# One up-weight load moved behind a token transpose, and eight matmul groups reordered to match, in a SwiGLU feed-forward kernel

## The chip, the core and the metric

The kernel runs on one core of a Trainium2 chip. The metric is device time in microseconds (us) of one execution; before the change it is 115.72 us, the median of 3 runs (115.47 to 116.23). Times inside the kernel are read from one profiled execution; "at 10.5" means 10.5 us after the start of its span.

## What is computed

```python
x: (1, 2048, 512)   w_gate, w_up: (512, 1376)   w_down: (1376, 512)   all bf16
def reference(x, w_gate, w_up, w_down):
    g = jax.nn.silu(x @ w_gate)
    u = x @ w_up
    return (g * u) @ w_down
```

## The kernel before

**Tiles.** The 2048 tokens are cut into 4 chunks of 512 (chunk 0 is tokens 0-511, chunk 1 is 512-1023). The 1376 hidden columns are 10 F tiles of 128 (F tile 0 to 9) and a rest of 96. A *group* is one PSUM bank: one F tile of one chunk, gate or up. In a *classic* pair (`classic`, L469) the gate group and the up group of an F tile are computed directly: ScalarE (ACT) takes silu of the gate bank into `sg_sb`, VectorE (DVE) multiplies it with the up bank into `h_sb`. In the first part such a group is 8 matmuls (L424), two 64-column halves for each of four 128-row slices of D, run as pairs side by side.

**Strassen part.** Most of the remaining work is done in units (`Unit`) of two F tiles by two chunks with seven products instead of eight (Winograd's form of Strassen's method). For these, sums and differences of weight blocks (`ss_sb`, `w_sums`, L545, on GpSimd, called POOL) and of token blocks (`tt_sb`, `x_sums`, L575, four sums T1 to T4) are needed. `tt0` is for chunks 0 and 1 and is made on DVE, in four instructions of about 1.2 us, each behind the one before. `ss_sb` sums of F tile pairs 2, 4 and 3 are made on POOL, each pair behind the last, and the first behind T4. A cast of one block (A22, and B22 of the tokens) runs on ACT (L541). Of the third pair, the cast on ACT waits for the last weight sum of that pair on POOL.

**Loads.** All loads are issued by SyncE (SP) in the order of the `load` calls: `load_w` (L267) brings a slab of two F tiles of gate or up weights, 256 KB; `load_x` (L279) is a DMA that transposes tokens into `xT_sb`, here 256 tokens, 256 KB at a time. The first loads are: x of tokens 0-255 (untransposed), gate slab 0-1 (`wg0`), x of 256-511 (`x0b`), up slab 0-1 (`wu0`), gate slab 2-3 (`wg2`), up slab 2-3 (`wu2`), then x of 512-767 (`x1a`) and 768-1023 (`x1b`). Each load has a semaphore of its own; those that matter here are dma21 (`wu0`), dma29 (`wg2`), dma20 (`wu2`), dma0 and dma1 (`x1a`, `x1b`), dma12 and dma28 (gate and up slab 4-5).

**What sets the order.** The program is written as a list of operations with reads and writes; `Plan.schedule` gives each operation to an engine. PE's and SP's operations keep the order in which they are written. Those of ACT, DVE and POOL are taken by a simulated list schedule, earliest possible start first, so their order depends on the estimated landing time of each load (`.land` in `load`) and on estimated costs. The result is a fixed order on each engine; at run time an engine waits at the head of its own queue.

**Around the change.** After the gates and ups of F tiles 0 and 1 of chunk 0, PE runs `classic(0, [2, 3])` (gate 2, gate 3, up 2, up 3 of chunk 0), then `classic(1, [ft])` for F tiles 0, 1 and 2 of chunk 1, then the rests of 96 columns (`plan_x` L488, `plan_y` L514), one more classic pair (L435), and the units (L616 and L628). The first group that reads chunk 1 is also the first that needs `x1a` and `x1b`; T1 on DVE needs them as well.

Of the kernel before, what the change touches and what calls it, by code (L numbers as in the profile page):

```python
# [168 lines left out]
def bass_standalone__swiglu_ffn__prompt_kernel(nc, x, w_gate, w_up, w_down, out):  # L169
    _, S, D = x.shape  # L170
    F = w_gate.shape[1]
    P = 128
# [26 lines left out]
    with ExitStack() as es:  # L199
# [40 lines left out]
        def take(i):  # L240
            rest.remove(i)
            return i
# [7 lines left out]
        plan = Plan()  # L250
        engines = {"P": nc.tensor, "S": nc.sync, "A": nc.scalar, "D": nc.vector, "G": nc.gpsimd}

        landed = 2700

        def load(name, emit, writes, busy, lag):
            nonlocal landed
            landed += lag
            i = take(homes[name] if name in homes else rest[0])
            plan.add("S", emit, writes=writes, busy=busy, lag=1800, dma=(i, 16)).land = landed + (300 if landed < 10500 else 1600)

        slabs = [(0, 2), (2, 4), (4, 6), (6, 8), (8, NFF + 1)]
        slab_of = {ft: a for a, b in slabs for ft in range(a, b)}

        def load_w(name, src, m, c0, f0, f1):
            load(
                name,
                lambda e: e.dma_start(  # L267
                    w_sb[:, :, m, c0:c0 + f1 - f0], src[:, f0:f1].rearrange("(k p) f -> p k f", p=P)
                ),
                [name], 600, 3.7 * (f1 - f0),  # L270
            )

        def load_slab(a, b):
            load_w(f"wg{a}", w_gate, 0, a * P, a * P, min(b * P, F))
            load_w(f"wu{a}", w_up, 1, a * P, a * P, min(b * P, F - 32))

        def load_x(name, t0, t1):
            load(
                name, lambda e: e.dma_start_transpose(xT_sb[:, :, t0:t1], xf[t0:t1, :]), [name], 1500, 4 * (t1 - t0)  # L279
            )  # L280

        load(
            "xn",
            lambda e: e.dma_start(
# [4 lines left out]
        load_w("wg0", w_gate, 0, 0, 0, slabs[0][1] * P)  # L289
        load_x("x0b", HT, SC)  # L290
        load_w("wu0", w_up, 1, 0, 0, slabs[0][1] * P)
        load_slab(*slabs[1])
        for i in range(2):
            load_x(f"x1{'ab'[i]}", SC + i * HT, SC + (i + 1) * HT)
        load_slab(*slabs[2])
        load_slab(*slabs[4])
        load_w("wut", w_up, 0, F, F - 32, F)
# [16 lines left out]
        for i in range(2):  # L314
            load(
                f"wdy{i}",
                lambda e, i=i: e.dma_start(wdt_sb[2 * R * i:2 * R * (i + 1), 0, :], w_down[NFF * P:F - R, :]),
# [12 lines left out]
        def silu_op(out, src, reads, writes, prio=5, busy=A_BUSY):  # L330
            return plan.add(
                "A", lambda e: e.activation(out, src, ACT.Silu), reads, writes, busy, A_LAG, prio  # L332
            )

        def tt_op(engs, out, a, b, alu, reads, writes, prio, busy, after=()):
            return plan.add(
                engs, lambda e: e.tensor_tensor(out, a, b, alu), reads, writes, busy,  # L337
                G_LAG if engs == "G" else D_LAG, prio, after=after,
            )
# [5 lines left out]
        def pe(emit, reads, writes, n, step=PE_STEP, after=()):  # L345
            return plan.add("P", emit, reads, writes, int(n * step), PE_LAG, dma=None, after=after)
# [60 lines left out]
        def next_bank():  # L407
            nonlocal n_group
            b = turn[n_group % NB]
            n_group += 1  # L410
            return b

        def x_keys(c):
            if c == 1:
                return ["x1a", "x1b"]
            if c:
                return [f"x{c}"]
            return [("x0a", dk) for dk in range(KD)] + ["x0b"]

        def gu_emit(m, ft, c, b, dks, n0, n1):  # L420
            def emit(e):
                for dk in dks:
                    for h in (0, HC):
                        ins = e.matmul(  # L424
                            psum[h:h + HC, b, n0:n1], lhsT=w_sb[:, dk, m, ft * P + h:ft * P + h + HC],
                            rhs=xT_sb[:, dk, c * SC + n0:c * SC + n1], start=(dk == 0), stop=(dk == KD - 1),
                            tile_position=(0, h),
                        )
                return ins
            return emit  # L430

        def gu_whole(m, ft, c, b):
            def emit(e):
                for dk in range(KD):
                    ins = e.matmul(  # L435
                        bank(b), lhsT=w_sb[:, dk, m, ft * P:(ft + 1) * P], rhs=xT_sb[:, dk, c * SC:(c + 1) * SC],
                        start=(dk == 0), stop=(dk == KD - 1),
                    )
                return ins
            return emit  # L440

        def gu_group(m, ft, c, b, whole=False):
            emit = gu_whole(m, ft, c, b) if whole else gu_emit(m, ft, c, b, range(KD), 0, SC)
            pe(emit, x_keys(c) + [f"w{'gu'[m]}{slab_of[ft]}"], [("b", b)], KD)
# [3 lines left out]
        def ring(name, tiles):  # L448
            n = rings.get(name, 0)
            rings[name] = n + 1  # L450
            i = n % len(tiles)
            return tiles[i][:, :], (name, i)

        def hview(ft, c):
            return (h0_sb, h1_sb)[c // 2][:, ft, c % 2 * SC:(c % 2 + 1) * SC]
# [8 lines left out]
        def classic_out(ft, c, bg, bu):  # L464
            sg, ksg = ring("sg", sg_sb)
            silu_op(sg, bank(bg), [("b", bg)], [ksg])
            tt_op("D", hview(ft, c), sg, bank(bu), ALU.mult, [ksg, ("b", bu)], [("h", ft, c)], 5, D_BUSY)

        def classic(c, fts, own=None):  # L469
            gates = [next_bank() for ft in fts] if own is None else own[:1]  # L470
            ups = [next_bank() for ft in fts] if own is None else own[1:]
            for ft, b in zip(fts, gates):
                gu_group(0, ft, c, b, own is not None)
            for ft, b in zip(fts, ups):
                gu_group(1, ft, c, b, own is not None)
            for ft, bg, bu in zip(fts, gates, ups):
                classic_out(ft, c, bg, bu)
# [61 lines left out]
        def cast_op(eng, out, src, reads, writes, prio, busy, after):  # L539
            plan.add(  # L540
                eng, lambda e: e.activation(out, src, ACT.Copy) if eng == "A" else e.tensor_copy(out, src),  # L541
                reads, writes, busy, A_LAG if eng == "A" else G_LAG, prio, after=after,
            )
# [31 lines left out]
        def x_sums(pi, eng, prio, after):  # L575

            c0, c1 = 2 * pi, 2 * pi + 1
            xk = x_keys(c0) + x_keys(c1)
            key = lambda n, k: ("tt", pi, X_SUM[n], k)
            last, first = after, None  # L580
            for n in ("T1", "T2", "T3", "T4"):
                behind = last
                last = []
                for k0, k1 in [(0, KH)] if pi == 0 else [(k, k + 1) for k in range(KH)]:
                    block = lambda k, c: xT_sb[:, k * KH + k0:k * KH + k1, c * SC:(c + 1) * SC]
                    at = lambda n: tt_sb[pi][:, X_SUM[n], k0:k1, :]
                    rd = lambda n: at(n).bitcast(FP32)
                    B11, B12, B21, B22 = (block(k, c) for k in range(2) for c in (c0, c1))
                    a, b, of_ = {
                        "T1": (B12, B11, ()), "T2": (B22, rd("T1"), ["T1"]),  # L590
                        "T3": (B22, B12, ()), "T4": (B21, rd("T2"), ["T2"]),
                    }[n]
                    last.append(tt_op(
                        eng, at(n), a, b, ALU.subtract, xk + [key(o, k) for o in of_ for k in range(k0, k1)],
                        [key(n, k) for k in range(k0, k1)], prio, 1160 if eng == "D" else 1250, behind,
                    ))
                first = first or last
            for k in range(KH):
                cast_op("A", tt_sb[pi][:, X_SUM["B22"], k, :], xT_sb[:, KH + k, c1 * SC:(c1 + 1) * SC], xk, [key("B22", k)], 8, A_BUSY, first if pi else ())
            return last  # L600
# [414 lines left out]
        units = [(pi, u) for pi in range(2) for u in U_ORDER[pi]]  # L1015
        early = [2 * u + i for u in range(NFF // 2) if u not in U_ORDER[0] for i in range(2)]
        sums = w_sums(0, 8, (), "A", True)
        classic(0, [2, 3])
        for ft in early[:3]:
            classic(1, [ft])  # L1020
        sums = x_sums(0, "D", 4, sums)
        for u in U_ORDER[0]:
            sums = w_sums(u, 2, sums, "A")
# [69 lines left out]
```

## Time and profile before

| quantity | value |
|---|---|
| median of the runs | 115.72 us |
| the profiled execution | 115.52 us |
| its span, first to last instruction | 114.2 us |
| outside the span | 1.3 us |
| PE busy | 110.7 us |
| DVE busy | 76.5 us |
| ACT busy | 64.0 us |
| POOL busy | 62.2 us |
| granted TensorE clock | 1.000 |

An engine's busy time is a sum over stages. The profile's chain of waits follows, from the last instruction backwards, what released each step; the waits list tells who stood idle for whom. In a row of the timeline stand start, busy time, engine, line, operation, tiles and count, and in brackets the idle time ahead of it with what ended it. A busy PE in this trace may still be a waiting one: a matmul whose operand is late shows as a longer piece, since its neighbours' modelled ends cover the gap.

### The profile page before, as it was taken

The page shows a single profiled execution, that of the slowest core. Times are in us where ns is not written, and L with a number is a line of the kernel's source. Part 1 is how long each engine was busy: PE and PEld are TensorE (multiplying, and loading weights), DVE is VectorE, ACT ScalarE, POOL GpSimd, SP SyncE. Part 2 cuts the span into 40 slices and gives each one's busy share as a digit, 9 for nine tenths or more (in the row PEclk, how much of TensorE's full clock was granted, in tenths as well). Part 3 has the DMA queues.
Part 4 walks back from the last instruction along what each step waited for, and adds up shares of the span by engine and source line. Part 5 has one row for each costly group of instructions (what it writes and reads, how often), then busy time and mean ns, then how long its engine had stood idle before and what let it go on. Part 6 is the DMA issues. An engine that isn't in the chain of part 4 may idle for free.

```text
span 114.2 us, 1765 instructions
## 1 busy us (share of the span) xinstructions
PE 110.7 (97%) x646; PEld 68.0 (60%) x654; DVE 76.5 (67%) x113; ACT 64.0 (56%) x123; POOL 62.2 (54%) x61
## 2 busy tenths in 40 slices
PE   7999999999999999999999999999999999999993
PEld 2665555456674858576776858653344557866452
DVE  0113799883956858493948668499999957486423
ACT  5344765866679895867678786740567960000000
POOL 1493004999999999999998999845000000000000
PEclk9999999999999999999999999999999999999999
DMA  3999999994000000000000000000031002227976
GB/s 101 235 276 237 321 190 225 271 361 101 0 0 0 3 0 3 0 0 6 0 3 0 0 0 0 0 0 0 17 127 46 0 0 46 46 52 183 201 200 197
DMA packets 22808, 9.84 MB, mean 86 GB/s; under 512 B 12848, under 2 KB 22672, under 8 KB 22800
## 3 DMA queue, kind: packets, MB, share of 16 engines
q1 hardware_dynamic: 20656, 8.69, 31.5%
q10 hardware_dynamic: 2144, 1.05, 3.2%
q8 instruction: 5, 0.08, 0.3%
q14 instruction: 3, 0.02, 0.1%
HBM read 4.75 MB, written 2.10 MB: 60 GB/s over the span
## 4 chain that ended last, share of the span: by engine, by line
PE 96%; DVE 1%; issue 1%
PE psum L616 32%; PE psum L726 15%; PE psum L628 12%; PE psum L424 11%; PE psum L864 10%; PE psum L876 4%; PE psum L488 3%; PE psum L754 3%; PE psum L350 2%; PE psum L435 2%; PE psum L514 2%; DVE o_sb L326 1%; PE psum L397 0%; PE psum L380 0%; PE psum L373 0%
## 5 line engine op out<-in xcount | busy, mean ns | idle before, releaser
L616 PE MATMUL psum<-tt_sb,ss_sb 128*128 128x512 f32 x160 | 40.0, 403 | 0.0
L616 PEld LDWEIGHTS psum<-tt_sb,ss_sb 128*128 128x128 f32 x160 | 29.7, 188 | 7.9 <-DVE ts_sb L337 0.6
L337 DVE TENSOR_TENSOR ts_sb<-r_sb,psum 128x512 f32<-128x512 f32 x32 | 20.6, 681 | 14.9 <-ACT r_sb L325 14.9
L337 POOL TENSOR_TENSOR h_sb<-sg_sb,ts_sb 128x512 bf16<-128x512 f32 x16 | 20.9, 1309 | 2.8 <-ACT sg_sb L332 2.8
L332 ACT ACTIVATE sg_sb<-psum 128x512 f32<-128x512 f32 x24 | 14.3, 599 | 11.2 <-PE psum L616 6.0
L325 ACT ACTIVATE r_sb<-psum 128x512 f32<-128x512 f32 x32 | 17.3, 594 | 4.5 <-PE psum L616 4.5
L337 DVE TENSOR_TENSOR h_sb<-sg_sb,psum 128x512 bf16<-128x512 f32 x24 | 16.3, 681 | 4.2 <-PE psum L424 3.9
L337 POOL TENSOR_TENSOR ss_sb<-w_sb 128x512 fp32r<-128x512 bf16 (+1 forms) x12 | 11.8, 997 | 12.6 <-DVE tt_sb L337 9.0
L726 PE MATMUL psum<-wd_sb,h_sb 128*128 128x512 bf16 (+2 forms) x98 | 17.9, 336 | 0.2 <-issue 0.2
L628 PE MATMUL psum<-xT_sb,w_sb 128*128 128x512 bf16 x59 | 14.2, 380 | 0.4 <-issue 0.2
L726 PEld LDWEIGHTS psum<-wd_sb,h_sb 128*128 128x128 bf16 x100 | 8.3, 98 | 9.2 <-issue 1.0
L424 PE MATMUL psum<-xT_sb,w_sb 128*64 128x512 bf16 (+1 forms) x128 | 12.8, 359 | 0.0
L332 ACT ACTIVATE sg_sb<-ts_sb 128x512 f32<-128x512 f32 x16 | 10.1, 634 | 1.6 <-DVE ts_sb L337 1.6
L424 PEld LDWEIGHTS psum<-xT_sb,w_sb 128*64 128x64 bf16 x128 | 7.3, 114 | 5.4 <-DMA w_sb<-in_w_up_dram 0.3
L628 PEld LDWEIGHTS psum<-xT_sb,w_sb 128*128 128x128 bf16 x64 | 5.5, 98 | 8.0 <-issue 2.5
L326 DVE COPY psum<-psum 128x512 f32<-128x512 f32 x8 | 5.6, 699 | 1.2 <-PE psum L616 0.5
L337 POOL TENSOR_TENSOR ss_sb<-w_sb,ss_sb 128x512 fp32r<-128x512 bf16 (+1 forms) x6 | 6.0, 1007 | 0.3
L337 POOL TENSOR_TENSOR ss_sb<-ss_sb,w_sb 128x512 fp32r<-128x512 f32 (+1 forms) x6 | 6.0, 1000 | 0.0
L326 DVE CAST o_sb<-psum 128x512 bf16<-128x512 f32 (+2 forms) x6 | 3.0, 512 | 4.2 <-PE psum L726 3.1
L337 POOL TENSOR_TENSOR ss_sb<-wd_sb 128x640 fp32r<-128x640 bf16 x4 | 5.6, 1406 | 0.0
L864 PE MATMUL psum<-tt_sb,ss_sb 128*128 128x512 f32 x20 | 5.6, 417 | 0.0
L864 PE MATMUL psum<-th_sb,ss_sb 128*128 128x512 f32 x20 | 5.5, 411 | 0.0
(72 smaller groups left out, 121.4 us busy)
## 6 DMA issues: line engine op xcount, KB each, us to landing
wd_sb<-in_w_down_dram SPq DMA_DIRECT2D x1, 1280.0 KB, 8.5
w_sb<-in_w_gate_dram SPq DMA_DIRECT2D x4, 256.0 KB, 4.0
w_sb<-in_w_up_dram SPq DMA_DIRECT2D x4, 256.0 KB, 4.2
out_dram<-o_sb SPq DMA_DIRECT2D x7, 128.0 KB, 1.8
out_dram<-xT_sb ACTq DMA_DIRECT2D x4, 128.0 KB, 2.5
out_dram<-xT_sb ACTq DMA_DIRECT2D x2, 256.0 KB, 3.2
w_sb<-in_w_gate_dram SPq DMA_DIRECT2D x1, 352.0 KB, 5.2
w_sb<-in_w_up_dram SPq DMA_DIRECT2D x1, 320.0 KB, 5.6
```

Source lines behind the costliest of these rows:

```text
L325: return e.activation(out, src, ACT.Copy)
L326: return e.tensor_copy(out, src)
L332: "A", lambda e: e.activation(out, src, ACT.Silu), reads, writes, busy, A_LAG, prio
L337: engs, lambda e: e.tensor_tensor(out, a, b, alu), reads, writes, busy,
L424: ins = e.matmul(psum[h:h + HC, b, n0:n1], lhsT=w_sb[:, dk, m, ft * P + h:ft * P + h + HC], rhs=xT_sb[:, dk, c * SC + n0:c * SC + n1], sta ...
L488: ins = e.matmul(psum[m:m + HC, b, :], lhsT=w_sb[:, dk, 0, XC0 + m:XC0 + m + HC], rhs=xT_sb[:, dk, c * SC:(c + 1) * SC], start=(dk == 0), ...
L616: ins = e.matmul(bank(dst), lhsT=s[:, k, :], rhs=t[:, k, :], start=(start and k == 0), stop=(k == KH - 1), skip_group_check=True,)
L628: ins = e.matmul(bank(dst), lhsT=w_sb[:, k0 + k, m, f:f + P], rhs=xT_sb[:, k0 + k, c:c + SC], start=(start and k == 0), stop=(k == KH - 1) ...
L726: ins = e.matmul(psum[:, b, 0:c1 - c0], lhsT=hrows(F_ORDER[n], t, 0, P), rhs=wd_sb[:, F_ORDER[n], c0:c1], start=(start and n == n0), stop= ...
L754: ins = e.matmul(bank(b), lhsT=lhsT, rhs=rhs, start=(start and n == 0), stop=(n == 2 and (kind == "T" or not start)), tile_position=(r0, 0 ...
L864: ins = e.matmul(bank(dst), lhsT=self.ds[s][:, j, self.q, :], rhs=self.dt[t][:, j, :], start=(start and n == 0), stop=(n == NFF // 2 - 1), ...
L876: ins = e.matmul(bank(dst), lhsT=wd_sb[:, 2 * j + a, d * P:(d + 1) * P], rhs=h0_sb[:, 2 * j + a, 0:SC], start=(n == 0), stop=(n == NFF // ...
```

## The change

Three edits are made. (1) On SP's queue the load of up slab 2-3 (`wu2`) moves behind the two transposes `x1a` and `x1b`. (2) The written order of PE changes: gate 2 and gate 3 of chunk 0 are followed by the classic pairs of F tiles 0 and 1 of chunk 1, and only then by up 2 and up 3 of chunk 0 with their multiplications; F tile 2 of chunk 1 comes after them as before. (3) The planner's estimate of a landing is 500 ns behind its running sum for every load, in place of 300 ns for the early ones and 1600 ns for those after 10.5 us. The third edit issues nothing by itself; it and the second change the order that the planner gives ACT, DVE and POOL.

```diff
-            plan.add("S", emit, ...).land = landed + (300 if landed < 10500 else 1600)
+            plan.add("S", emit, ...).land = landed + 500
...
-        load_slab(*slabs[1])
+        load_w("wg2", w_gate, 0, 2 * P, 2 * P, 4 * P)
         for i in range(2):
             load_x(f"x1{'ab'[i]}", SC + i * HT, SC + (i + 1) * HT)
+        load_w("wu2", w_up, 1, 2 * P, 2 * P, 4 * P)
         load_slab(*slabs[2])
...
-        classic(0, [2, 3])
-        for ft in early[:3]:
+        held = [(ft, next_bank()) for ft in (2, 3)]
+        for ft, b in held:
+            gu_group(0, ft, 0, b)
+        for ft in early[:2]:
             classic(1, [ft])
+        for ft, b in held:
+            up = next_bank()
+            gu_group(1, ft, 0, up)
+            classic_out(ft, 0, b, up)
+        classic(1, early[2:3])
```

(`early` is F tiles 0, 1, 2, 3.) Line numbers after the change are one higher in most of the kernel.

On SP's queue, from the up slab 0-1 on, this is the difference; `x2` is a count of two instructions, `x1a` and `x1b`.

```order
 L267 DMA w_sb<-in_w_up_dram 128x4x256
 L267 DMA w_sb<-in_w_gate_dram 128x4x256
+L279 DMA_TRANSPOSE xT_sb<-in_x_dram 128x4x256 x2
 L267 DMA w_sb<-in_w_up_dram 128x4x256
-L279 DMA_TRANSPOSE xT_sb<-in_x_dram 128x4x256 x2
 L267 DMA w_sb<-in_w_gate_dram 128x4x256
 L267 DMA w_sb<-in_w_up_dram 128x4x256
```

The two transposes take the place of `wu2` in the queue, and `wu2` stands behind them and still ahead of slab 4-5.

On PE these are the rows from the gates of F tiles 2 and 3 on, before the change. A row without a wait holds the matmuls that follow the waiting one; 16 matmuls are two groups.

```order
L424 MATMUL psum<-xT_sb,w_sb 64x512 [waits s_dma29]
L424 MATMUL psum<-xT_sb,w_sb 64x512 x15
L424 MATMUL psum<-xT_sb,w_sb 64x512 [waits s_dma20]
L424 MATMUL psum<-xT_sb,w_sb 64x512 x15
L424 MATMUL psum<-xT_sb,w_sb 64x512 [waits s_dma1,s_dma0,s_A]
L424 MATMUL psum<-xT_sb,w_sb 64x512 x7
L424 MATMUL psum<-xT_sb,w_sb 64x512 [waits s_D]
```

And these are the rows of the same place after it.

```order
L425 MATMUL psum<-xT_sb,w_sb 64x512 [waits s_dma29]
L425 MATMUL psum<-xT_sb,w_sb 64x512 x15
L425 MATMUL psum<-xT_sb,w_sb 64x512 [waits s_dma1,s_dma0]
L425 MATMUL psum<-xT_sb,w_sb 64x512 x15
L425 MATMUL psum<-xT_sb,w_sb 64x512 [waits s_A]
L425 MATMUL psum<-xT_sb,w_sb 64x512 x7
L425 MATMUL psum<-xT_sb,w_sb 64x512 [waits s_D]
L425 MATMUL psum<-xT_sb,w_sb 64x512 x7
L425 MATMUL psum<-xT_sb,w_sb 64x512 [waits s_dma20,s_A]
```

PE's wait for the two transposes has moved two groups earlier, and its wait for `wu2` four groups later.

On DVE these are the rows from the multiplications of F tiles 0 and 1 of chunk 0 to the last of the four token sums, before the change; `h0_sb<-sg_sb2` and `sg_sb3` are F tiles 2 and 3 of chunk 0, `sg_sb4` and `sg_sb5` F tiles 0 and 1 of chunk 1.

```order
L337 TENSOR_TENSOR tt0_sb<-xT_sb 128x1024 [waits s_dma1,s_G,s_dma0]
L337 TENSOR_TENSOR h0_sb<-sg_sb2,psum 128x512 [waits s_P,s_A]
L337 TENSOR_TENSOR tt0_sb<-xT_sb,tt0_sb 128x1024 [waits s_D]
L337 TENSOR_TENSOR h0_sb<-sg_sb3,psum 128x512 [waits s_P,s_A]
L337 TENSOR_TENSOR tt0_sb<-xT_sb 128x1024 [waits s_D]
L337 TENSOR_TENSOR h0_sb<-sg_sb4,psum 128x512 [waits s_A,s_P]
L337 TENSOR_TENSOR tt0_sb<-xT_sb,tt0_sb 128x1024 [waits s_D]
```

After the change the buffers go by the new order: `sg_sb2` and `sg_sb3` are F tiles 0 and 1 of chunk 1, `sg_sb4` and `sg_sb5` F tiles 2 and 3 of chunk 0.

```order
L338 TENSOR_TENSOR tt0_sb<-xT_sb 128x1024 [waits s_G,s_dma1,s_dma0]
L338 TENSOR_TENSOR tt0_sb<-xT_sb,tt0_sb 128x1024 [waits s_D]
L338 TENSOR_TENSOR h0_sb<-sg_sb2,psum 128x512 [waits s_A,s_P]
L338 TENSOR_TENSOR tt0_sb<-xT_sb 128x1024 [waits s_D]
L338 TENSOR_TENSOR h0_sb<-sg_sb3,psum 128x512 [waits s_P,s_A]
L338 TENSOR_TENSOR tt0_sb<-xT_sb,tt0_sb 128x1024 [waits s_D]
L338 TENSOR_TENSOR h0_sb<-sg_sb4,psum 128x512 [waits s_P]
```

T1 and T2 now stand back to back, and one multiplication fewer stands between T1 and T4.

More of the change, by code (lines that the diff above doesn't have):

```diff
@@ L258, in load @@
             i = take(homes[name] if name in homes else rest[0])
-            plan.add("S", emit, writes=writes, busy=busy, lag=1800, dma=(i, 16)).land = landed + (300 if landed < 10500 else 1600)
+            plan.add("S", emit, writes=writes, busy=busy, lag=1800, dma=(i, 16)).land = landed + 500
         slabs = [(0, 2), (2, 4), (4, 6), (6, 8), (8, NFF + 1)]
```

## The prediction

> **What bounds the kernel now.** I read the page first: its busy times and its chain that ended last.
>
> ```profile
> span 114.2 us, 1765 instructions
> PE 110.7 (97%) x646; PEld 68.0 (60%) x654; DVE 76.5 (67%) x113; ACT 64.0 (56%) x123; POOL 62.2 (54%) x61
> PE 96%; DVE 1%; issue 1%
> ```
>
> PE is the bound from end to end: 96% of the chain is PE's own work. The change neither adds nor removes a matmul, so it can win only where PE works slower than it could. The second view, the chain in order of time, shows where that is. Its columns are start, length and count.
>
> ```profile
> 6.94 0.03 issue
> 6.97 10.55 PE psum L424 x96
> 17.52 1.73 PE psum L488 x16
> ...
> 22.70 0.16 issue
> ...
> 36.34 4.77 PE psum L616 x20
> ...
> 42.85 4.63 PE psum L616 x20
> ...
> 49.22 4.57 PE psum L616 x20
> ```
>
> The rows of one shape are to be compared. L488 has the same 64-column matmuls as L424 and takes 1.73/16 = 0.108 us each; 96 at that rate are 10.38, so L424 lost 0.17. Of the pieces of 20 at L616, the one at 36.34 took 4.77 against 4.57 at 49.22, a loss of 0.20; that at 42.85 lost 0.06. With the 0.16 at 22.70 this is 0.59 us in all: the most that any better arrival of operands could return in the stages that the change touches or feeds.
>
> The third view, the waits from 33 to 37.5, names the cause of the 0.20.
>
> ```profile
> DVE ts_sb L337 <- ACT r_sb L325: 2.4, 1, 2.4
> ACT ss_sb L541 <- POOL ss_sb L337: 0.6, 1, 0.6
> PEld psum L616 <- DVE ts_sb L337: 0.6, 2, 0.3
> ```
>
> Read upwards from PE: PE's weight loads stood for DVE's `ts_sb`, DVE for ACT's copies `r_sb`, and ACT for a weight sum on POOL. The timelines of POOL and ACT say why POOL was late.
>
> ```profile
> 9.01 0.68 POOL L337 TENSOR_TENSOR ss_sb<-w_sb,ss_sb 128x256 fp32r<-128x256 bf16 x1
> 18.69 2.27 POOL L337 TENSOR_TENSOR ss_sb<-w_sb 128x512 fp32r<-128x512 bf16 x2 [9.01 <-DVE tt_sb L337]
> 32.92 1.17 POOL L337 TENSOR_TENSOR ss_sb<-w_sb,ss_sb 128x512 fp32r<-128x512 bf16 x1
> 32.45 1.08 ACT L325 ACTIVATE r_sb<-psum 128x512 f32<-128x512 f32 x2
> 34.13 0.72 ACT L541 ACTIVATE ss_sb<-w_sb 128x256 fp32r<-128x256 bf16 x2 [0.60 <-POOL ss_sb L337]
> ```
>
> POOL stood 9.0 us for the last token sum T4, then worked without a pause to 32.92 + 1.17 = 34.09, and ACT's cast, at the head of its queue from 32.45 + 1.08 = 33.53, could start only then. T4 itself hangs on the landing of `x1b`:
>
> ```profile
> 12.12 1.23 DVE L337 TENSOR_TENSOR tt_sb<-xT_sb 128x1024 fp32r<-128x1024 bf16 x1 [2.43 <-DMA xT_sb<-in_x_dram]
> 13.26 0.68 DVE L337 TENSOR_TENSOR h_sb<-sg_sb,psum 128x512 bf16<-128x512 f32 x1
> 17.33 1.22 DVE L337 TENSOR_TENSOR tt_sb<-xT_sb,tt_sb 128x1024 fp32r<-128x1024 bf16 x1
> ```
>
> **The change, step by step.** *The transposes land earlier.* SP's issues, and the times from issue to landing, for `x0b`, `x1a` and `x1b` in this order, with `wu2` between:
>
> ```profile
> L279 SPq DMA_TRANSPOSE xT_sb<-in_x_dram x1: 1329/1329/1329, 1.7 to 1.7; - x1
> DMA to landing us min/median/max: 3.6/3.6/3.6
> ...
> 4.21 0.51 SPq L267 DMA_DIRECT2D w_sb<-in_w_up_dram  x1
> L279 SPq DMA_TRANSPOSE xT_sb<-in_x_dram x1: 2149/2149/2149, 4.8 to 4.8; - x1
> DMA to landing us min/median/max: 4.8/4.8/4.8
> 6.95 1.51 SPq L279 DMA_TRANSPOSE xT_sb<-in_x_dram  x1
> DMA to landing us min/median/max: 5.0/5.0/5.0
> ```
>
> `x1a` is now issued at 4.21. An issue took 1.33 (`x0b`) to 2.15 us (`x1a`), so `x1b` is issued at 5.6 to 6.4, and lands 3.6 to 5.0 later: between 9.2 and 11.4, against 6.95 + 5.0 = 11.95 before. Which is nearer is told by the state of the DMA engines, in a table of stages (last columns: clock, DMA share, GB/s) and in the list of DMA queues from 9.5 to 10.5.
>
> ```profile
> 9.50:10.00 0.50, 0.50 (x8) 0.23 (x4) 0.19 (x1) 0.21 (x1) 0.18 (x1) 1.00 1.31 259
> 10.00:10.50 0.50, 0.50 (x8) 0.28 (x6) 0.00 (x0) 0.39 (x1) 0.00 (x0) 1.00 0.42 76
> q8 instruction: 1, 0.02, 6.7%
> ```
>
> The engines were full until 10.0 and nearly done by 10.5, so the bytes of `x1b` were in by about 10.5, except where one packet of instructions sat: 6.7% of 16 engines for 1 us is 1.07 us on one engine. I read the rest of the 11.95 as that engine's delay. With `wu2` gone from ahead, `x1b` moves by 0.55 (the step of SP's queue from 4.21 to 4.76) up to 1.0 us (256 KB at 259 GB/s). I take the smaller and get 10.5 - 0.55 = 9.95, if the packet falls elsewhere.
>
> [...]
>
> *PE needs them earlier.* Before the first chunk-1 group stood 48 matmuls from 6.97, at 10.55/96 = 0.11 each: 12.25, with 0.3 us to spare behind 11.95. Now 32 stand before it: 10.5. To 9.95 the slack is 0.55; at the late bound of 11.4 PE stands 0.9 us, and everything on PE stands behind it, ACT's silu `sg_sb5` behind its cast, DVE's multiplications behind T1. I take no wait. `wu2` is issued after `x1b`, at about 7.9, and with the 4.5 us that `wu4` took it lands at 12.4; its first use is now after 64 matmuls, at 14.0: nothing, with 1.6 to spare. The loads from slab 4-5 on keep their issue times, since what stands ahead of them is the same.
>
> *DVE.* T1 starts at 9.95, behind POOL's last early sum (9.01 + 0.68 = 9.69). T1 and T2 end at 12.4, a multiplication at 13.1, T3 at 14.3. The next multiplication waits for ACT, whose silu now stands behind two casts of slab 4-5:
>
> ```profile
> L267 SPq DMA_DIRECT2D w_sb<-in_w_up_dram x1: 507/507/507, 9.1 to 9.1; - x1
> DMA to landing us min/median/max: 4.5/4.5/4.5
> 13.14 0.40 ACT L541 ACTIVATE ss_sb<-w_sb 128x256 fp32r<-128x256 bf16 x1
> 13.45 0.58 ACT L332 ACTIVATE sg_sb<-psum 128x512 f32<-128x512 f32 x1
> ```
>
> Slab 4-5 is complete at 9.13 + 4.5 = 13.6, the cast at 14.0, the silu at 14.6, the multiplication at 15.3, T4 at 16.5. Before it was 17.33 + 1.22 = 18.55: 2.05 earlier.
>
> *POOL and ACT.* POOL's chain moves by 2.05, less some 0.3 for its first multiplication, whose silu on ACT comes no sooner: the sum that ended at 34.09 ends at about 32.3, and ACT at 33.53 finds it done. The 0.60 goes whole, with 1.2 us to spare, so it would go even if `x1b` came 1 us later than I take it. `r_sb` and `ts_sb` come 0.6 earlier and PE, which lost 0.20 behind them, takes 4.57 for that piece. What is late next there is nothing by more than the 0.06 at 42.85. The later POOL order puts each unit's multiplication one pair of token sums (2.3 us) further back; with 2 us of lead this costs 0.3 at most, and no row of the waits shows DVE or PE standing for such a product, so I count nothing.
>
> *The rest* costs nothing: matmuls, casts and multiplications are the same in number and shape; the multiplications that free the early groups' PSUM banks end by 18.5 by the steps above, and the first reuse that waits for one of them is a `plan_x` group, behind 17.52. The 0.16 at 22.70 is a change of shape on PE and stays, and so does the wait for `wu0` at 6.94.
>
> **Sum.** 115.52 (span 114.2 and 1.3 around it) - 0.20 = 115.3 against the profiled execution. That lies 0.2 under the median of 115.72. The 0.3 us that `x1b` had to spare before may explain part of the scatter of the runs, but nothing shows it, so I keep half of the 0.2 and predict **115.4**.
>
> **Rivals.** *One: nothing comes of it.* The wait on POOL goes, but PE's piece at 36.34 finds another partner late (ACT now does both token casts ahead of a silu, 0.64 us more in one place). For it: ACT is busy 7.1 of the 7.4 us there:
>
> ```profile
> 34.60:42.00 7.40, 7.34 (x32) 4.65 (x32) 4.95 (x9) 7.11 (x15) 7.40 (x7) 1.00 0.00 1
> ```
>
> Against it: ACT gains the same 0.60 first. Time: 115.7.
>
> *Two, slower: `x1b` is late for PE.* It decides from a landing after 10.5. It takes only that the packet of instructions falls on `x1b` again, as at 9.5 to 10.5 before. The price is 0.9 us at a landing of 11.4 and 1.45 at the old 11.95; less 0.2 that is gained all the same, 116.4 to 117.0 on the median. [...] Against it: the bytes of `x1b` are then due 0.5 us before it. [...]
>
> *Three: more than I count.* All of the 0.59 comes back, and the scatter with it: 114.9.
>
> **How the numbers follow.** The forecast gets 0.56 (115.2 to 115.6), nothing 0.20, late transposes 0.17, more 0.07. The range reaches from 114.9 (115.52 less 0.59) to 116.4 (the nearer end of rival two) and leaves out about 1 in 10. 1% of 115.72 is 1.16 us, about what a measurement of this kernel can tell from no change. Faster by that takes more than all the 0.59 that I can see: 0.03. Slower takes a stall of 1.4 us, the far end of rival two (0.07), or a wait that I don't see (0.03): 0.10. Within 1%: 0.87.
>
> **What will show it.** POOL's 9.0 us wait shrinks to about 7; the wait of ACT's `ss_sb` cast for POOL is gone; the piece of L616 near 36 takes 4.57; DVE's first token sum starts near 10. A wait of PE's weight load for `in_x_dram` near 10.5 would show rival two; a wait for `in_w_up_dram` near 14 would prove the landing of `wu2` wrong. The prediction is wrong if a wait of over 0.3 us stands between 10 and 12 on PE, or if the piece near 36 is still above 4.7.

## The result, and the profile after

| kernel | median us (runs) | ratio to before, 95% interval | profiled execution, span |
|---|---|---|---|
| before | 115.59 (21) | | 115.52, 114.2 |
| changed | 115.09 (21) | 0.9962 [0.9947, 0.9977] | 114.94, 113.6 |

The changed kernel is 0.4% faster, 0.44 us by the ratio (0.27 to 0.61). That is within the 1% that counts as no change here, but the interval lies clear of 1. A second measurement of the same kernel gave 0.9961 [0.9943, 0.9979]. All ratios leave out the executions that ran in a slower state; with the loads alone (below) these were four of six, at a granted clock of 0.986, so its ratio rests on two.

First the transposes. These are SP's issues, DVE's first and last token sums T1 and T4, and POOL's first sum behind T4, in the timeline of the changed kernel.

```profile
4.21 3.21 SPq L279 DMA_TRANSPOSE xT_sb<-in_x_dram  x2
7.46 0.58 SPq L267 DMA_DIRECT2D w_sb<-in_w_up_dram  x1
...
9.97 1.23 DVE L338 TENSOR_TENSOR tt_sb<-xT_sb 128x1024 fp32r<-128x1024 bf16 x1 [0.62 <-POOL ss_sb L338]
...
14.70 1.22 DVE L338 TENSOR_TENSOR tt_sb<-xT_sb,tt_sb 128x1024 fp32r<-128x1024 bf16 x1
...
15.99 2.27 POOL L338 TENSOR_TENSOR ss_sb<-w_sb 128x512 fp32r<-128x512 bf16 x2 [6.16 <-DVE tt_sb L338]
```

T1 starts at 9.97 and not 12.12, and what releases it is no longer the DMA but POOL: `x1b` was complete at 9.59, POOL's last early sum only at 9.84, so the last 0.38 of the 0.62 us in the bracket is POOL's. T4 ends at 15.92 instead of 18.55, and POOL's wait shrinks from 9.0 to 6.2 us.

Then what that lead does at 33 us, where ACT stood for POOL. These are POOL's last sum of the third pair with the multiplication ahead of it, and ACT's cast that waits for that sum.

```profile
29.83 1.29 POOL L338 TENSOR_TENSOR h_sb<-sg_sb,ts_sb 128x512 bf16<-128x512 f32 x1 [0.83 <-ACT sg_sb L333]
31.07 1.18 POOL L338 TENSOR_TENSOR ss_sb<-w_sb,ss_sb 128x512 fp32r<-128x512 bf16 x1
...
32.19 1.08 ACT L326 ACTIVATE r_sb<-psum 128x512 f32<-128x512 f32 x2
33.15 0.73 ACT L542 ACTIVATE ss_sb<-w_sb 128x256 fp32r<-128x256 bf16 x2
```

The sum ends at 32.25 (34.09 before), the cast has no bracket and so no wait. T4 came 2.63 us earlier and the sum only 1.84, since the multiplication stood 0.83 us for ACT's silu. And the chain in order of time shows what PE makes of it.

```profile
4.91 12.27 PE psum L425 x128
17.18 1.73 PE psum L489 x16
18.91 0.86 PE psum L515 x8
19.77 1.82 PE psum L489 x16
...
36.06 4.56 PE psum L617 x20
40.61 1.74 PE psum L629 x8
42.36 4.56 PE psum L617 x20
46.91 1.74 PE psum L629 x8
```

The pieces of 20 near 36, 42 and 49 us took 4.77, 4.63 and 4.57 before and take 4.56 now (the third in the whole chain, at 48.66): 0.21 + 0.07 + 0.01 = 0.29 us. One thing is new: the second piece of 16 at L489 takes 1.82 against 1.73 for the first. The waits from 4 to 22 us name it: `x3`, the transpose of tokens 1536-2047 and the last of the transposes.

```profile
PEld psum L489 <- DMA xT_sb<-in_x_dram: 0.4, 1, 0.4
...
PEld psum L425 <- DMA w_sb<-in_w_up_dram: 0.2, 1, 0.2
```

### The profile page after: what moved, and what is told of

Same layout as the page of the kernel before. It is cut to its first block, busy times and chain, and to the rows that moved or that the text cites. A ratio compares the mean times of both kernels' runs of the same rounds, so it can differ in the third digit from the quotient of the medians.

```text
span 113.6 us, 1771 instructions
## 1 busy us (share of the span) xinstructions
PE 110.8 (98%) x654; PEld 67.9 (60%) x654; DVE 76.8 (68%) x113; ACT 63.7 (56%) x123; POOL 62.3 (55%) x61
## 2 busy tenths in 40 slices
DMA packets 22808, 9.84 MB, mean 87 GB/s; under 512 B 12848, under 2 KB 22672, under 8 KB 22800
## 4 chain that ended last, share of the span: by engine, by line
PE 97%; DVE 1%; issue 0%
PE psum L617 32%; PE psum L727 15%; PE psum L629 12%; PE psum L425 11%; PE psum L865 10%; PE psum L877 4%; PE psum L489 3%; PE psum L755 3%; PE psum L351 2%; PE psum L436 2%; PE psum L515 2%; DVE o_sb L327 1%; PE psum L374 0%; PE psum L381 0%; PE psum L398 0%; PE psum L354 0%
## 5 line engine op out<-in xcount | busy, mean ns | idle before, releaser
L333 ACT ACTIVATE sg_sb<-psum 128x512 f32<-128x512 f32 x24 | 14.3, 599 | 9.4 <-PE psum L617 6.0
L727 PE MATMUL psum<-wd_sb,h_sb 128*128 128x512 bf16 (+2 forms) x100 | 18.4, 337 | 0.0
L629 PE MATMUL psum<-xT_sb,w_sb 128*128 128x512 bf16 x64 | 15.4, 381 | 0.0
L727 PEld LDWEIGHTS psum<-wd_sb,h_sb 128*128 128x128 bf16 x100 | 8.3, 98 | 9.2 <-issue 1.0
L425 PE MATMUL psum<-xT_sb,w_sb 128*64 128x512 bf16 (+1 forms) x128 | 12.4, 353 | 0.0
L333 ACT ACTIVATE sg_sb<-ts_sb 128x512 f32<-128x512 f32 x16 | 10.1, 633 | 1.4 <-DVE ts_sb L338 1.4
```

The costliest lines, as they stand in the source:

```text
L425: ins = e.matmul(psum[h:h + HC, b, n0:n1], lhsT=w_sb[:, dk, m, ft * P + h:ft * P + h + HC], rhs=xT_sb[:, dk, c * SC + n0:c * SC + n1], sta ...
L629: ins = e.matmul(bank(dst), lhsT=w_sb[:, k0 + k, m, f:f + P], rhs=xT_sb[:, k0 + k, c:c + SC], start=(start and k == 0), stop=(k == KH - 1) ...
L727: ins = e.matmul(psum[:, b, 0:c1 - c0], lhsT=hrows(F_ORDER[n], t, 0, P), rhs=wd_sb[:, F_ORDER[n], c0:c1], start=(start and n == n0), stop= ...
```

## The experiments

The expectations name their theories themselves; a letter means what is said beside it. Two questions were open: is POOL's lead what the change is worth, and does the landing of `x1b` cost PE anything by itself?

**Both kernels once more**, unedited, so that each has a second profile.

> The kernel before, unchanged, as a control and as a second profile. Two losses of PE were read in the first profile: up slab 0-1 landed at 6.93 and PE's matmuls on it began at 6.97, against 6.58 and 6.63 after the change (0.34 us), and the piece of 20 matmuls near 36 took 4.77 against 4.56 (0.21 us), behind ACT's 0.60 us wait for POOL. Theory A (half of the gain is POOL's lead, half is a steady earlier start on up slab 0-1): the second profile shows PE at 6.9 to 7.0 again and 4.77 near 36. Theory B (POOL's lead is all that is steady; the landing of up slab 0-1 scatters whatever stands behind it): 4.77 near 36 again, but a start anywhere between 6.5 and 7.0. Ratio to the kernel before under both: 1.000.

> The changed kernel, unchanged, as a control and as a second profile. Ratio to the kernel before about 0.996 (115.09 to 115.59 in the first comparison). Theory A: PE starts on up slab 0-1 at 6.6 to 6.7 again. Theory B: the start may come anywhere between 6.5 and 7.0. Both: the piece near 36 takes 4.56 and ACT has no wait for a POOL sum there. The packet of instructions lay at 13.05 and delayed the gate slab 8-9 and, through SP's queue, x of tokens 1536-2047, for which PE lost 0.07 us near 20.5; if it falls elsewhere this loss is gone.

Measured: 0.999 [0.9971, 1.0008] and 0.9961 [0.9943, 0.9979]. This is the chain of before in its second profile.

```profile
6.93 5.37 PE psum L424 x48
12.30 0.08 issue
12.38 5.37 PE psum L424 x48
...
36.57 4.83 PE psum L616 x20
41.39 1.74 PE psum L628 x8
43.14 4.62 PE psum L616 x20
```

The pieces of 4.83 and 4.62 are there again. But the 96 matmuls that were one piece of 10.55 in the first profile are broken in two: the last pair ahead of `x1b` starts at 11.92, the next only at 12.38, 0.461 us later where the others are 0.216 apart. PE lost 0.25 us to `x1b`, which was complete only at 12.24. So the 0.3 us that `x1b` was read to have to spare is not there in every execution. It was not there in the first either: PE's first pair on `x1b` started at 12.17, and where PE did wait for that load it started 0.14 us behind the landing (12.38 behind 12.24), so the landing at 12.00 left 0.04. The changed kernel's second profile has `x1b` at 9.70 and its three pieces at 4.56. Its `wu0` landed at 6.96 and PE began on it at 7.26, so the steady earlier start of theory A falls.

**The cast on ACT freed, in before.** The third pair's cast no longer waits for POOL's last sum:

```diff
-                    after if casts == "G" else () if slot < 3 else [last],
+                    after if casts == "G" else (),
```

> The kernel before, in which the ACT cast of the third pair's block no longer waits for POOL's last sum of that pair (the cast only reads weights, into a buffer that nothing else uses yet); the loads and PE's order stay. Theory A and B: ACT's 0.60 us wait goes, the piece near 36 takes 4.56, and the time falls by 0.2 to 0.3 us (ratio 0.9975 to 0.998), without the transposes landing any earlier. Rival theory C (the whole gain of the change comes from the loads, and the POOL wait is covered by other work): ratio 1.000.

Measured: 0.9988 [0.9969, 1.0007], which excludes neither the expected gain nor none. The piece near 36 is 4.69, not 4.56. ACT's timeline shows why.

```profile
38.11 0.63 ACT L541 ACTIVATE tt_sb<-xT_sb 128x512 fp32r<-128x512 bf16 x1 [0.88 <-POOL tt_sb L337]
```

The wait has moved to the next cast that stands behind POOL, where it was 0.29 us before. POOL is late by its whole chain, so a single edge that is cut only shows the next.

**POOL made later, in the changed kernel.** The first sum of the first pair is made four times over (three extra sums of about 1.2 us, 3.6 us in all; the planner's cost of each is cut to a quarter so that no order changes):

```diff
-                for n in ("S1", "S2", "S3", "S4"):
+                for n in ("S1",) * (4 if u == U_ORDER[0][0] else 1) + ("S2", "S3", "S4"):
...
```

> The changed kernel with POOL's first sum of F tile pair 4-5 computed four times instead of once: three more instructions of about 1.2 us each right behind T4, at an unchanged order on PE, ACT and DVE. POOL's last sum of the third pair, which ended at 32.25, then ends near 35, and ACT, there at 33.15, waits 1.7 us. Theory A and B: PE loses about 0.4 us less than that wait (0.60 cost it 0.21 before), so 1.2 to 1.4 us: 116.3 to 116.5, ratio to the kernel before about 1.007. Theory C: no loss, 0.996.

Measured: 1.0122 [1.0091, 1.0153], more than the 1.007 that was expected. The waits from 33 to 37.5 us are those of before, and larger.

```profile
DVE ts_sb L338 <- ACT r_sb L326: 3.9, 1, 3.9
ACT ss_sb L542 <- POOL ss_sb L338: 2.0, 1, 2.0
PEld psum L617 <- DVE ts_sb L338: 1.7, 1, 1.7
PE psum L617 <- DVE ts_sb L338: 1.2, 1, 1.2
```

3.6 us of delay became 2.0 us of waiting on ACT. Most of the rest is what POOL has to spare in the changed kernel: the 0.83 us for which it stood for the silu, and the 0.90 between the end of its sum at 32.25 and the cast at 33.15. Beyond that POOL holds up PE. Against the changed kernel in the same measurement (0.9961) the loss is 1.6% or 1.9 us (1.2 to 1.4 expected).

**POOL's lead alone, in before.** One sum of the third pair goes from POOL to DVE; loads and PE's order stay:

```diff
-                        "G", part(n), a, b, alu, ...
+                        "D" if n == "S3" and u == U_ORDER[0][2] else "G", part(n), a, b, alu, ...
```

> Before with one sum of the third pair's weights (S3, 1.17 us) moved from POOL to DVE, into the 1.9 us for which DVE waits for ACT near 26.5 us; loads and PE's order stay. It gives POOL about what the change gave it (its last sum of that pair ended 1.8 us earlier there), and nothing else. Theory A (POOL's lead is the 0.2 us that was forecast, and the rest of the gain is x1b, which is late in the old order): the chain's piece near 36 us takes 4.56 and not 4.77 to 4.83, no wait of ACT for POOL ahead of it, x1b still lands at 12.0 to 12.5 with PE waiting 0 to 0.25 us for it, and the ratio is 0.997 to 0.999, between before and the changed kernel. Rival (POOL's lead is worth nothing by itself, as when the cast alone was freed): the piece stays above 4.65, ratio 0.999 to 1.001.

Measured: 0.9985 [0.996, 1.001], which does not separate the two by time. The chain of its profile does.

```profile
36.77 4.56 PE psum L617 x20
41.33 1.74 PE psum L629 x8
43.07 4.56 PE psum L617 x20
```

With the old loads and the old order on PE, about one sum less on POOL brings both pieces to 4.56. The waits from 33 to 37.5 us hold no wait for POOL any more. The planner also put one of the third pair's two casts on ACT earlier in this kernel, so the edit is not POOL's alone. But all the profiles point the same way: these pieces take 4.56 to 4.58 in the eight in which POOL is early, and more in the four in which it is late. So the 0.29 us is POOL's lead, whatever gives it. (The profiled run, 116.18, was the longest of the twelve: from the start of its L727 piece to the end it took 10.14 us against 9.57 to 9.60 in the other profiles, for a reason that no view shows.)

**Each half of the change alone.** The first kernel has the new loads and the old order on PE; the second has the new order on PE and the old loads, and was measured twice. Both keep the third edit.

```diff
-        held = [(ft, next_bank()) for ft in (2, 3)]
...
+        classic(0, [2, 3])
+        for ft in early[:3]:
```

> The changed order of loads with the old order on PE: wu2 lands behind x1b, at 10.3 to 11.3 us by the changed profiles (10.69), while PE wants it at about 10.4 (the third gate-and-up pair of the first chunk). PE waits 0 to 0.9 us there. x1b lands by 9.7 and is wanted at 12.1, so no stall there (0 to 0.24 us in before's profiles), and POOL's and DVE's sums of x1b start some 2 us earlier as in the changed kernel, so the wait of ACT for POOL near 36 us goes (0.2). Theory that both parts are needed: ratio 1.000 to 1.004. Rival, that PE's new order buys nothing and the loads do it all: 0.995 to 0.997, with wu2 in time.

```diff
-        load_w("wg2", w_gate, 0, 2 * P, 2 * P, 4 * P)
+        load_slab(*slabs[1])
...
-        load_w("wu2", w_up, 1, 2 * P, 2 * P, 4 * P)
```

> The changed order on PE with the old order of loads: wu2 goes ahead of x1a and x1b again. PE now needs x1b at about 10.5 us instead of 12.1. The old loads landed x1b at 12.00, 12.24 and 12.47 us, in each case with the instruction packet on the scalar queue at 9.86 to 10.22 us. Theory A (only POOL's lead counts, x1b's last part comes when the packet lets it): POOL's sums still start late or early with x1b, and PE waits for x1b from 10.5 to 12.0-12.4, so 1.5 to 1.9 us are lost: 117.1 to 117.5 us, ratio 1.013 to 1.016. Theory B (the packet comes with PE's own place in its instructions, and so at 12.7 us with the changed PE order, as in the two changed profiles): x1b lands at 10.5 to 10.7, PE waits 0.0 to 0.3 us, T1 starts at about 10.9, and the time is between the changed kernel's and before's: ratio 0.997 to 1.001.

> PE's changed order with the old loads once more, since its first profile had wu0 land at 7.76 us (6.6 to 7.0 elsewhere), which hid what PE waits for at x1b. If that landing was chance: wu0 lands by 7.0, PE needs x1b at about 10.5, x1b lands at 10.5 to 10.7 with the packet behind 12 us, so PE waits 0 to 0.3 us, the piece near 36 us takes 4.56 to 4.65, and the profiled run takes 115.3 to 115.8 us. If wu0 is late again, the order of the loads or of PE is its cause and the ratio of 1.000 is that lateness. Ratio 0.997 to 1.001 in either case.

Measured: the loads alone 1.0118 [1.0088, 1.0149], slower than expected; PE's order alone 1.000 [0.9979, 1.002] and 0.9979 [0.9958, 1.0001]. These are PE's timeline and the DMA queues from 8.5 to 9.5 us with the loads alone.

```profile
12.40 1.92 PE L425 MATMUL psum<-xT_sb,w_sb 128*64 128x512 bf16 x16 [1.84 <-DMA w_sb<-in_w_up_dram]
```

```profile
q8 instruction: 1, 0.02, 9.6%
```

In the old order PE wants `wu2` behind 32 matmuls, at 10.4; up to 0.9 us of waiting was expected, and it started at 12.40, 2.0 us late (the bracket counts 1.84, from the modelled end of the matmul before). `wu2` was complete at 12.36, although 15 of its 16 parts were in by 10.73. I take it that the sixteenth stood behind the instruction packet: 9.6% of 16 engines for 1 us is 1.5 us on one engine, and the packet began at 9.01. The price that the prediction's second rival put on `x1b` fell, and more, on the load that had taken its place. So the loads need PE's order.

The reverse half keeps POOL's part of the gain in its profiles; by time it keeps nothing in one measurement and about half in the other, and the intervals reach from none to all. In its second profile the chain reads as follows.

```profile
5.92 4.88 PE psum L424 x56
10.80 0.01 issue
10.81 7.10 PE psum L424 x64
```

`x1b` landed at 10.68, PE started on it at 10.81 and lost 0.18 (one step between matmuls of 0.397 instead of 0.216). T1 starts at 10.8 and all three pieces take 4.56. The first profile had `x1b` at 11.24 and T1 at 11.37, with 0.09 lost to `x1b`, and lost 0.9 us at `wu0` (7.76, against 6.6 to 7.1 in all other profiles that load it at this place). The second shows the late `wu0` as chance; how many of the runs behind the 1.000 had it is not known.

**The planner's old estimate in the changed kernel**, which on ACT only moves one silu ahead of a cast:

```diff
-            ... .land = landed + 500
+            ... .land = landed + (300 if landed < 10500 else 1600)
```

> The changed kernel with the planner's old estimate of landings; that moves one silu of F tile 3 ahead of a cast of ACT and nothing on PE. If the loads' order and PE's order hold all of the gain: ratio to before 0.996, 115.1 to 115.6 us, as the changed kernel. If the estimate's effect on ACT's order were part of it, the ratio would be 0.998 or above.

Measured: 0.9972 [0.9953, 0.9991]; the pieces near 36 and 43 take 4.56. The third edit adds nothing that shows. But its profile has the largest loss to `x3`.

```profile
16.87 4.32 DMA xT_sb<-in_x_dram
21.18 0.04 issue
21.23 1.05 PE psum L489 x8
```

**A candidate beyond the change.** `wu0` loads ahead of `x0b`, and the ups of F tiles 0 and 1 of tokens 0-255 run ahead of tokens 256-511:

```diff
-            load_x("x0b", HT, SC)
...
+            load_x("x0b", HT, SC)
...
```

> A candidate on top of the change: wu0 loads ahead of x0b, and the ups of F tiles 0 and 1 of tokens 0-255 run ahead of tokens 256-511. In the changed kernel PE has done the first gates and waits for wu0, which lands at 6.6 to 7.0 us, by 0.1 to 0.4 us. Here the work of the first two tiles is in the order of its landings, so that wait should go. Theory that this wait is on the path: 0.1 to 0.3 us better than the changed kernel, ratio to before 0.994 to 0.996. Rival, that the bytes landed set the end of the first two tiles whatever their order, so that the wait only moves to x0b: ratio 0.996 as the changed kernel.

Measured: 1.0038 [1.001, 1.0067]. In its profile (115.46, span 114.1) the wait for `wu0` is gone, and the instruction packet, at 9.20, met `wu2`: complete at 12.24, it cost PE nothing. But four of its twelve runs took 115.3 to 115.7 and eight 116.4 to 116.8. The profile is of the shorter kind, so what the longer ones wait for stays open. Even the shorter ones, 115.47 on average or 0.998 of before in the same measurement, don't beat the changed kernel.

**The packet in all twelve profiles.** These are the landings of whole loads, the start of the first instruction packet, and what PE lost, from start to start of its matmuls. PE's order is that of the groups that the change moves, and `wg8` is the gate slab 8-9.

| profile | PE's order | packet at | load with one part late: 15 of 16 parts, all | PE lost to it | `x3` landed | PE lost to `x3` | pieces near 36, 43, 49 |
|---|---|---|---|---|---|---|---|
| before | old | 9.86 | `x1b` 10.49, 12.00 | 0 | 19.81 | 0 | 13.97 |
| before, again | old | 10.13 | `x1b` 10.68, 12.24 | 0.25 | 20.55 | 0 | 14.02 |
| cast freed | old | 10.22 | `x1b` 10.88, 12.47 | 0.18 | 20.24 | 0 | 13.83 |
| sum on DVE | old | 10.03 | `x1b` 10.43, 12.09 | 0 | 20.06 | 0 | 13.68 |
| loads alone | old | 9.01 | `wu2` 10.73, 12.36 | 2.01 | 20.64 | 0 | 13.68 |
| changed | new | 13.05 | `wg8` 13.88, 15.56 | 0 | 20.49 | 0.09 | 13.68 |
| changed, again | new | 12.71 | `wg8` 14.18, 15.23 | 0 | 20.35 | 0 | 13.68 |
| old estimate | new | 13.01 | `wg8` 14.44, 16.02 | 0 | 21.18 | 0.35 | 13.68 |
| PE's order alone | new | 14.31 | none that stands out | 0 | 21.55 | 0 | 13.68 |
| the same, again | new | 14.04 | none that stands out | 0 | 21.34 | 0.24 | 13.68 |
| POOL later | new | 12.70 | `wg8` 14.49, 15.42 | 0 | 20.40 | 0 | POOL holds up PE |
| the candidate | new, other start | 9.20 | `wu2` 11.55, 12.24 | 0 | 20.30 | 0 | 13.70 |

Where the halves are exchanged one at a time, the packet's time goes with PE's order and not with the loads: 9.0 to 10.2 us in five profiles of the old order, 12.7 to 14.3 in six of the new. The candidate breaks the rule: it has the new order of these groups, with other matmuls and another order of loads ahead of them, and its packet is at 9.20. In the ten rows that name a load, one of its 16 parts comes 0.7 to 1.7 us after the others. (The views call the packet's queue q8 and name no engine; that it is the scalar queue, as an expectation has it, they don't show.)

## Why the prediction was right, point by point

The forecast was 115.4, the median is 115.09; the difference of the medians is 0.50, where 0.32 was forecast. The median lies just under the 115.2 to 115.6 that got 0.56; the forecast started from 115.72, and before was 115.59 over 21 runs. The mechanism held, with some steps that were mis-sized or right by luck.

- **`x1b` lands at 9.95**: 9.59 to 9.73 in the three profiles of the changed loads and order. Of its two bounds for the move, 0.55 and 1.0 us, the prediction took the smaller; the fifteenth of the 16 parts of `x1b` moved by 0.92, from 10.49 to 9.57.
- **The packet falls elsewhere**: it did; rival two took it to come near 10 again. It came 3 us later with the new order on PE, at 12.71 to 13.05 in the three profiles of the changed kernel against 9.86 and 10.13 in the two of before. What sets its time, no run shows. Had it stayed at 10, it would have met `wu2`, as with the loads alone, and `wu2` at 12.4, its landing there, would still be ahead of its use at 14.0: the new order has room for it in either place. The candidate's profile shows that case, with the packet at 9.20 and no loss.
- **PE needs `x1b` at 10.5 and finds it**: PE came to it at 10.1 to 10.7, with no wait in any profile of the changed kernel. `wu2` landed at 10.69 to 11.71, ahead of the 12.4 forecast, which had borrowed the 4.5 us of a later load.
- **T4 ends at 16.5**: 15.92. T1 started at 9.97, within 0.02 of the forecast, but by luck: POOL's early sum at 9.84 set it, forecast for 9.69, and not `x1b`. Slab 4-5 was complete at 12.92 and not at 13.6, so DVE had no wait for ACT up to T4.
- **POOL's sum ends at about 32.3 and ACT's 0.60 goes whole**: 32.25, and it went. That the end agrees to 0.05 is luck: T4 came 0.6 earlier than forecast, and the multiplication ahead of the sum waited 0.83 for ACT's silu (0.92 and 1.28 in the two other profiles) where 0.3 was forecast. 0.90 was left to spare, not 1.2. 0.20 was forecast for the piece near 36, 0.21 came.
- **"What is late next there is nothing by more than the 0.06 at 42.85"**: that 0.06 was the same lateness of POOL and went too. The term is 0.29, not 0.20; the kernel with one sum on DVE has all of it with the old loads and the old order on PE.
- **"so L424 lost 0.17"**: nothing was lost. From 7.21 on, pairs of matmuls start every 0.216 us without a gap up to the first of L488 at 17.35; the piece ends at 17.52 by the modelled end of its last matmul. In the changed kernel 96 matmuls take the same 10.55, from 6.63 to 17.18. Nor did the 0.16 behind them go. So of the 0.59 of rival three 0.33 could not come back, and the other 0.26, POOL's, did.
- **"The 0.3 us that `x1b` had to spare before may explain part of the scatter ..., but nothing shows it"**: this is the step that was mis-sized. The 0.3 was 0.04 by PE's own starts. In the four executions of the old loads and order PE lost 0, 0.25, 0.18 and 0 to `x1b`, 0.11 on average, and the change removes that.
- **"The rest costs nothing"**: not quite. `x3` lands at 20.35 to 21.18 instead of 19.81 to 20.55, and PE lost 0.09, 0 and 0.35 to it in the three profiles of the changed kernel (the third with the old estimate), about 0.15. In the table it is latest where the packet came latest; but the two profiles with the new loads and the packet at 9 have `x3` at 20.64 and 20.30, against 20.35 to 20.49 in three of the four with the packet on slab 8-9. So the packet is not shown to be the cause, and it stays open.
- **The POOL order costs nothing, the wait for `wu0` stays**: no wait shows a cost of the first, and the second stayed in two of the three profiles (0.14 and 0.62 us; in the third PE came after the landing).

The sum of what was seen is 0.29 + 0.11 - 0.15 = 0.25 us; the ratio gives 0.44 (0.27 to 0.61). The terms outside POOL are means over three or four executions that scatter by 0.3, so the remaining 0.2 can't be assigned. Of the rivals, "nothing comes of it" fell, and "late transposes" was seen only with half of the change (0.09 and 0.18 us with PE's order alone).

## What to carry to other kernels

A wait seen at one edge may be the lateness of a whole engine: cutting the edge moved the wait to the next cast (0.88 us there, the piece near 36 at 4.69), while giving that engine one sum less, or an earlier start, removed all of it (4.56). Moving a load and moving its use belong together: here PE's order alone measured 1.000 and 0.998 where both together gave 0.996, and the loads alone cost 1.2%. The slack of 0.3 us read in one profile was no slack here, where `x1b` landed at 12.00 to 12.47 in four profiles of the same loads and order; read it from the start of the matmul that uses the load, and look at a second profile before counting on it.

## What the hardware did that was not expected

**One part of a load landed 0.7 to 1.7 us behind the others where a 16 KB instruction packet had run.** The first such packet of an execution took 0.94 to 1.53 us, and in ten of twelve profiles one of the load's 16 parts came 0.7 to 1.7 us after the others; the load is complete only with its last part: in the first profile of before 15 parts of `x1b` were in by 10.49, the sixteenth at 12.00, and T1 started at 12.12. That this part stood on the packet's DMA engine is read from the times, and no view names the engine. The first packet cost PE 0 to 0.25 us with the old loads and order, and 2.0 us with the loads alone. The four later ones start at 26.78, 53.48, 81.23 and 101.86 us in the first profile of before and at 25.92, 52.67, 80.72 and 101.37 in that of the changed kernel; in neither do the waits there show an engine standing for a load. What calls for the first at 9 to 10 us in some programs and at 13 to 14 in others, no run shows.

**PE started at half speed, for a time that varied.** These are PE's first group matmuls in two executions of the same changed kernel, first and second profile; the columns are stretch, busy time and count on PE, granted clock, DMA share and GB/s.

```profile
4.70:5.30 0.60, 0.56 (x12) 1.00 1.11 211
5.30:5.90 0.60, 0.60 (x16) 1.00 1.14 299
```

```profile
4.70:5.30 0.60, 0.59 (x6) 1.00 0.85 172
5.30:5.90 0.60, 0.60 (x10) 1.00 0.98 239
```

Twelve matmuls stand against six in the same 0.6 us. From start to start a pair took 0.213 us at first and 0.109 later; the step came at 4.69 us in the first profile, at 6.38 in the second, and at 4.6 to 6.7 in the others (5.36 in the first of before). The granted clock of 1.00 in both rows, and the 1.000 over the whole span, miss it: the trace's record of full clock begins only at 4.55 in the first profile and at 6.35 in the second (5.35 in the first of before), and the view counts the time without a record as full. Nine of the twelve traces have such a record, and in each it begins within 0.15 us of the step. In the second profile PE so came to the first ups at 7.26 and not at 6.63, and its 128 matmuls took 12.86 us against 12.27 (of the 0.63, a `wu0` that landed at 6.96 and not at 6.58 would have cost some 0.4 by itself). What sets the step, no run shows; over the twelve profiles it moved by 2.1 us. The 0.59 between these two executions of one kernel is more than the whole effect of the change, so one execution of each kernel would have told nothing of its time.
